# Reading a filter's mirrored rows by DMA from GpSimd's queue instead of turning them on TensorE

## The chip, the cores and the metric

The kernel runs on one core of a Trainium2 chip. The core has TensorE (PE, matrix products; its weight loads are shown as PEld), VectorE (DVE), ScalarE (ACT), GpSimd (POOL) and SyncE (SP), each with an instruction queue of its own that runs in order, and DMA engines that move data between the device memory and the on-chip memory SBUF. TensorE writes to PSUM, from which ScalarE or VectorE copies. The metric is device time in microseconds of one execution. The median of 3 runs of the kernel before is 134.64 us (133.65, 134.64, 134.67).

## The reference

Two branches share the input `x` of 2048 rows by 512 columns (bf16) and are mixed by a gate for each row:

```python
def _A_ref(x, w_r, w_i):                  # spectral filter
    X = rfft2(x.astype(float32), axes=(-2, -1))
    X = X * (w_r + 1j * w_i)              # w_r, w_i: 2048 x 257
    return irfft2(X, s=(S, D), axes=(-2, -1)).astype(bfloat16)

def _B_ref(x, w1, b1, w2, b2):            # MLP over the rows
    h = _layernorm(x, axis=-1)
    u = _gelu(einsum("bsd,sf->bdf", h, w1) + b1)        # f: 1792
    return (einsum("bdf,fs->bds", u, w2) + b2).transpose(0, 2, 1)

g = sigmoid((x * gate_w).sum(-1, keepdims=True))
out = g * _A_ref(A_x, ...) + (1 - g) * _B_ref(A_x, ...)
```

## The kernel before, in words

The MLP is 224 matmuls of 512 columns for `w1` (L656, PSUM tiles `acc` and `fb`), a GELU on ScalarE (L670), and 224 more for `w2` (L932). The Fourier transforms are made of matmuls with tables of cosines and sines and of radix-4 steps on VectorE:

- Over the rows: a radix-4 step on `x` (L494 to L501), then matmuls (`fa`, L513 to L516) with the table `ta`, copied into `X` by ScalarE (L519).
- Over the columns: radix-4 steps on `X` (L526 to L533, L552 to L568), then matmuls (L621 to L624), copied into `B` by ScalarE (L628).
- The product with the filter: sums and differences of `B` (L769, L770), four products with `W` (L777), combinations (L782 to L791). A few lines at the edge of the spectrum are done apart: `sp`/`fx`, `c0`/`cm`/`ce`, `nyq` with the filter row `wn`.
- The inverse: radix-4 steps, matmuls with `ti` (L838 to L845) and then `tg` (L913 to L917), folds (L937 to L941) and the mixing with the MLP's output (L952, L958, L970).

Because the input is real, the product for the spectral row k needs the filter's rows k + 512 e and their mirror images 512 (e + 1) - k, for e = 0 to 3. `W` holds both: `W[p, component, lt, e, s, column]`, with lt = 0 for even rows k and lt = 1 for odd ones, s = 0 for the row itself and s = 1 for its mirror. Before, even rows lie in rising order: partition p below 64 holds k = 4p, the others k = 2 + 4 (p - 64). So the mirrored rows are needed in falling order. For lt = 0 they are loaded in rising order into `wt`, and TensorE turns them with the reversed unit matrix `flip`: eight matmuls of 256 columns (L706) and four of 2 (L716), which ScalarE copies into `W` (L710, L719). For lt = 1 the DMA itself reads rows backwards, 32 at a time:

```python
for e in range(4):
    dma(W[:, 1, e, 1, 0:257], v[:, 3 - e, 3, :].rearrange("(o i) l -> o i l", o=4)[:, ::-1])
```

All filter loads stand on SyncE's queue, 18 for each of the two components (`ld_W`, L413). All DMAs go through the helper `dma` in L303, so all have that line in the profile; its third argument can name another engine's queue. `wprep` (L724) halves the filter's row 0 and makes sums of its end columns; it needs all of `W`.

The order of the work comes from a planner (`Plan`, L137). Each task has an engine, a cost in us, the keys it reads and writes, PSUM tiles to take or give back, and a priority (a smaller number goes first). The planner plays the tasks through with these costs, each engine taking the ready task of the smallest number, and the instructions are issued in the order found. So the order is fixed before the run: an engine that reaches an instruction whose data are not there waits, whatever stands behind it. Waits between engines and DMAs are added by the framework from what the instructions read and write.

SyncE's order around the change: the inputs and first weights, `gw`, the filter's first component (priority 17), four loads of `wb` (22), the second component (25), `ti` (28), `tg` (29), then the loads of `w2` (31 and above).

Of the kernel before, what the change touches and what calls it, by code (L numbers as in the profile page):

```python
# [16 lines left out]
P = 128  # L17
S = 2048
# [12 lines left out]

def ti_at(r):
    return (0, 1024, 512, 1920)[r], (512, 896)[r % 2]


def make_tables():
# [10 lines left out]
    for r in range(4):  # L47
        s = 4 * p + r
        for n, k0 in enumerate((0, 2)):
            th = ang(s, k0 + 4 * np.arange(64), S)  # L50
            ta[:, r, n * 128:n * 128 + 64] = np.cos(th)
            ta[:, r, n * 128 + 64:n * 128 + 128] = -np.sin(th)
        ta[:, r, 64] = alt
# [5 lines left out]
        k = np.where(p < 64, 4 * p, 2 + 4 * (p - 64))  # L59
        o, w = ti_at(r)  # L60
        v = ti[:, o:o + w]
        if r % 2:
            sg = np.where(p < 64, 1.0, -1.0)[:, None]
# [6 lines left out]
            v[0, 2:4] = alt * (0.5 ** 0.5 if r == 1 else -(0.5 ** 0.5))  # L70
# [5 lines left out]
        else:  # L76
            s5 = np.append(s, 512)
            for lt, kk in enumerate((k, 1 + 4 * (p ^ 96))):
                th = ang(kk, s5, S)
                c, n = np.cos(th), -np.sin(th)  # L80
                if lt == 0:
                    n[0, 0:P] = 0.0 if r == 0 else -alt
# [4 lines left out]
    ti[0, 2816:2945] = np.append(alt, 1.0)  # L87
# [174 lines left out]
def kernel(  # L262
# [42 lines left out]
    def alloc_first():  # L305
# [17 lines left out]
        t["wn"] = sb([1, 2, WL], BF16, "wn")  # L323
        t["ta"] = sb([P, 4, 640], BF16, "rot")
        t["wt"] = sb([P, 2, 4, WL], BF16, "wt")
# [87 lines left out]
    def ld_W(comp):  # L413
        v = wsrc[comp].rearrange("(e c k) l -> c e k l", e=4, k=4)
        z = wsrc[comp].rearrange("(v u w) l -> w u v l", v=4, u=2)

        def emit():
            W, u = t["W"][:, comp], t["wt"][:, comp]
            dma(u[64:127, :, 0:257], v[65:128, :, 0, :])
            dma(u[0:64, :, 0:257], v[64:128, :, 2, :])  # L420
            dma(u[127:128, 0:2, 0:257], z[0:1, 1, 2:4, :])
            dma(u[127:128, 2, 0:257], wsrc[comp][1536:1537, :])
            dma(u[127:128, 3, 0:257], wsrc[comp][0:1, :])
            for e in range(4):
                dma(W[:, 1, e, 1, 0:257], v[:, 3 - e, 3, :].rearrange("(o i) l -> o i l", o=4)[:, ::-1])
            for o in range(4):
                dma(W[32 * o:32 * o + 32, 1, :, 0, 0:257], v[96 - 32 * o:128 - 32 * o, :, 1, :])
            dma(W[1:64, 0, :, 0, 0:257], v[1:64, :, 0, :])
            dma(W[64:128, 0, :, 0, 0:257], v[0:64, :, 2, :])
            for i in range(2):  # L430
                dma(W[0:1, 0, 2 * i:2 * i + 2, 0, 0:257], z[0:1, i, 0:2, :])
            dma(t["wn"][:, comp, 0:257], wsrc[comp][1024:1025, :])
        return emit

    for comp in range(2):
        add("SP", 9.0 - 2 * comp, ld_W(comp), writes=[("W", comp), ("wt", comp)], prio=17 + 8 * comp, nbytes=300000, after=[a0])
        if comp == 0:
            load_wb(1)
# [8 lines left out]
    for r in range(4):  # L447
# [60 lines left out]
        for dq in range(4):  # L508
            def fa(r=r, dq=dq):
                pa = t["pa", r, dq] = ps([P, 2, 2, P], F32, "fa", 2)  # L510
                ta = t["ta"][:, r, :]
                w = lambda k: t["xf", r][:, k, dq * P:(dq + 1) * P]
                T.matmul(pa[:, 1], lhsT=w(2), rhs=ta[:, 256:512], start=True, stop=False)  # L513
                T.matmul(pa[:, 1], lhsT=w(3), rhs=ta[:, 384:640], start=False, stop=True)
                T.matmul(pa[:, 0, :, 0:64], lhsT=w(0), rhs=ta[:, 0:128], start=True, stop=True)
                T.matmul(pa[:, 0, :, 64:128], lhsT=w(1), rhs=ta[:, 128:256], start=True, stop=True)  # L516
# [59 lines left out]
    def sp0():  # L576
        V.tensor_copy(t["sp"][:], t["X"][:, 0, :, :, :, 0])
# [25 lines left out]
    add("DVE", 0.15, lambda: V.tensor_copy(t["X"][:, 0, :, :, :, 0], t["fx"][:]), reads=["fx"],  # L603
# [94 lines left out]
    for comp in range(2):  # L698
        for lt in (0,):
            for a in range(2):  # L700
                tag = ("fa", "fb")[a]

                def wf(comp=comp, lt=lt, a=a, tag=tag):
                    pw = t["pw", comp, lt, a] = ps([P, 2, L], F32, tag, 2)
                    for i in range(2):
                        T.matmul(pw[:, i], lhsT=t["flip"][:], rhs=t["wt"][:, comp, 3 - 2 * a - i, 0:L], start=True, stop=True)  # L706
                add("PE", mm(256, 256), wf, reads=[("wt", comp), "flip"], writes=[("pw", comp, lt, a)], prio=5, alloc=[tag])

                def wfe(comp=comp, lt=lt, a=a):
                    A.copy(t["W"][:, comp, lt, 2 * a:2 * a + 2, 1, 0:L], t["pw", comp, lt, a][:])  # L710
                add("ACT", act(512), wfe, reads=[("pw", comp, lt, a)], writes=[("W~", comp, lt)], prio=3, free=[tag])

    def wfn():
        pw = t["pwn"] = ps([P, 4, 2], F32, "fa", 2)
        for e in range(4):
            T.matmul(pw[:, e], lhsT=t["flip"][:], rhs=t["wt"][:, :, 3 - e, 256], start=True, stop=True)  # L716
    add("PE", mm(*[4] * 4), wfn, reads=[("wt", 0), ("wt", 1), "flip"], writes=["pwn"], prio=5, alloc=["fa"])
    wtk = [("W~", comp, 0) for comp in range(2)]
    add("ACT", 0.3, lambda: A.copy(t["W"][:, :, 0, :, 1, 256], t["pwn"][:].rearrange("p e k -> p k e")),  # L719
        reads=["pwn"], writes=wtk, prio=3, free=["fa"])  # L720
# [3 lines left out]
    def wprep():  # L724
        W, pm = t["W"], t["wpm"]
        V.tensor_scalar_mul(W[0:1, :, 0, 0, :, 0:257], W[0:1, :, 0, 0, :, 0:257], 0.5)
# [4 lines left out]
    add("DVE", 0.8, wprep, reads=[], writes=[("W", 0), ("W", 1), "wpm"] + wtk, prio=1)  # L731
# [283 lines left out]
```

## Time and profile before

| | |
|---|---|
| median of 3 runs | 134.64 us |
| the profiled execution, its own time | 134.46 us |
| its span, first to last instruction | 132.6 us |
| PE busy | 124.6 us (94%), 769 matmuls |
| DVE busy | 115.3 us (87%), 295 instructions |
| ACT busy | 80.5 us (61%), 155 instructions |
| POOL busy | 0.2 us, 4 instructions |
| DMA | 23.18 MB, all on the queues of SyncE (q1) and ScalarE (q10) but for code |
| granted TensorE clock | 1.00 throughout |

Times inside the profile are us from the first instruction. "Busy" is the time in which an engine had an instruction running; matmuls overlap, so one of 512 columns is shown with 0.37 us but follows the last by 0.216. The idle time in front of an instruction is put down to what released it: another engine's instruction, a DMA, or "issue". The chain that ended last goes back from the last instruction, at each step to what it waited for. DMA share is the mean busy share of the 16 DMA engines.

### The profile page before, as it was taken

Reading aid. Unit: us, or ns where it says so; the run is one execution under the profiler, and the core shown is the slowest. Engines: PE = TensorE matmul, PEld = TensorE weight load, DVE = VectorE, ACT = ScalarE, POOL = GpSimd, SP = SyncE. Lnnn points to the kernel's source line nnn. Section 1 sums busy time; section 2 is a strip of 40 time slices with the busy share of each in tenths; the row PEclk is TensorE's granted clock in tenths of the full one; section 3 lists DMA queues with packets and bytes.
Section 4 is the critical chain, followed back from the end, with each engine's and each line's share of the span. In section 5 each row is a group of like instructions: output and inputs, shape, how many; then the busy total and the mean of one; then the engine's idle time right before and its main releaser. Section 6 shows DMA issues by size and latency. Waiting matters only on the chain.

```text
span 132.6 us, 2193 instructions
## 1 busy us (share of the span) xinstructions
PE 124.6 (94%) x769; PEld 70.7 (53%) x783; DVE 115.3 (87%) x295; ACT 80.5 (61%) x155; POOL 0.2 (0%) x4
## 2 busy tenths in 40 slices
PE   6749999999999999999999999999999999999991
PEld 2234464545544566744445544556865766655590
DVE  2987999999999997389999999999598599999841
ACT  4036699999999999972222016235994857755200
POOL 0000000000000000000000000000000000000000
PEclk9999999999999999999999999999999999999999
DMA  4899999925499565999964930000000003034031
GB/s 133 245 370 394 393 380 371 321 60 134 90 309 342 96 134 131 337 373 413 421 253 72 420 146 2 0 2 5 0 0 0 5 0 158 23 135 161 2 119 40
DMA packets 17350, 23.18 MB, mean 175 GB/s; under 512 B 1446, under 2 KB 14780, under 8 KB 17340
## 3 DMA queue, kind: packets, MB, share of 16 engines
q1 hardware_dynamic: 16780, 22.39, 49.8%
q10 hardware_dynamic: 560, 0.66, 1.6%
q8 instruction: 6, 0.10, 0.3%
q14 instruction: 4, 0.03, 0.1%
HBM read 20.93 MB, written 2.10 MB: 174 GB/s over the span
## 4 chain that ended last, share of the span: by engine, by line
PE 80%; DVE 10%; DMA 6%; SPq 1%; issue 1%
PE acc L932 35%; PE acc L656 25%; DMA x<-in_A_x_dram 6%; DVE stats L462 4%; PE fb L656 3%; PE fa L838 1%; PE fb L838 1%; PE fa L624 1%; PE fb L624 1%; SPq L303 1%; DVE mv L463 1%; DVE gl L495 1%; DVE st L494 1%; PE fa L513 1%; DVE nmr L477 1%
## 5 line engine op out<-in xcount | busy, mean ns | idle before, releaser
L932 PE MATMUL acc<-gl,wb 128*128 128x512 bf16 (+1 forms) x123 | 30.5, 373 | 0.3
L656 PE MATMUL acc<-h,wb 128*128 128x512 bf16 x124 | 28.8, 379 | 0.2
L932 PE MATMUL acc<-gl,wa 128*128 128x512 bf16 (+1 forms) x94 | 23.2, 372 | 0.1
L932 PEld LDWEIGHTS <-wb 128*128 128x128 bf16 x144 | 14.9, 114 | 10.7 <-DMA wb<-in_B_w_dram 0.6
L952 ACT ACTIVATE x<-acc,ombb,omg 128x512 bf16<-128x512 f32 x14 | 10.7, 778 | 15.5 <-PE acc L932 15.4
L656 PEld LDWEIGHTS <-wb 128*128 128x128 bf16 x128 | 12.4, 97 | 13.5
L656 PE MATMUL acc<-h,wa 128*128 128x512 bf16 x62 | 16.8, 379 | 1.2 <-DVE stats L462 0.7
L932 PEld LDWEIGHTS <-wa 128*128 128x128 bf16 x108 | 11.7, 114 | 8.5
L656 PEld LDWEIGHTS <-wa 128*128 128x128 bf16 x96 | 9.1, 98 | 10.3 <-DMA wa<-in_B_w_dram 0.9
L670 ACT ACTIVATE gl<-acc,b1f 128x512 bf16<-128x512 f32 x12 | 8.5, 708 | 9.6 <-PE acc L656 9.6
L462 DVE BATCH_NORM_STATS2 stats<-x 128x6 f32<-128x512 bf16 x16 | 10.8, 673 | 2.8 <-DMA x<-in_A_x_dram 2.8
L519 ACT CAST X<-fa 128x512 bf16<-128x512 f32 x16 | 8.8, 583 | 3.9 <-PE fa L516 3.8
L486 ACT ACTIVATE h<-x,nmr,rstd 128x512 bf16<-128x512 bf16 x13 | 9.8, 805 | 1.2 <-DVE nmr L477 1.2
L684 ACT ACTIVATE x<-x 128x512 bf16<-128x512 bf16 x16 | 10.2, 672 | 0.0
L923 ACT ACTIVATE eo<-fa,g 128x512 bf16<-128x512 f32 x8 | 5.5, 688 | 6.7 <-DVE x L958 5.0
L656 PE MATMUL fb<-h,wa 128*128 128x512 bf16 x31 | 9.0, 379 | 0.0
L513 PE MATMUL fa<-rot,gl 128*128 128x256 bf16 x16 | 4.3, 272 | 2.1 <-DMA rot<-dft_ta 2.1
L353 PE MATMUL fa<-xp 128*128 128x512 bf16 x13 | 4.4, 514 | 1.2 <-DVE xp L314 1.2
L923 ACT ACTIVATE eo<-fb,g 128x512 bf16<-128x512 f32 x8 | 5.5, 686 | 0.0
L958 DVE TENSOR_TENSOR x<-x,eo 128x512 bf16<-128x512 bf16 x14 | 5.4, 418 | 0.0
L628 ACT CAST B<-fb 128x512 bf16<-128x512 f32 x8 | 5.2, 651 | 0.0
L628 ACT CAST B<-fa 128x512 bf16<-128x512 f32 x8 | 5.1, 639 | 0.0
(170 smaller groups left out, 227.3 us busy)
## 6 DMA issues: line engine op xcount, KB each, us to landing
wb<-in_B_w_dram SPq DMA_DIRECT2D x8, 512.0 KB
wb<-in_B_w_dram SPq DMA_DIRECT2D x4, 1024.0 KB
wa<-in_B_w_dram SPq DMA_DIRECT2D x3, 1024.0 KB
wa<-in_B_w_dram SPq DMA_DIRECT2D x3, 768.0 KB
x<-in_A_x_dram SPq DMA_DIRECT2D x3, 512.0 KB
out_dram<-x SPq DMA_DIRECT2D x3, 512.0 KB
rot<-dft_ti SPq DMA_DIRECT2D x1, 736.5 KB
rot<-dft_ta SPq DMA_DIRECT2D x4, 160.0 KB
```

What stands on the lines that cost most here:

```text
L462: V.bn_stats(out=t["stats"][:, j, :], in_=t["x"][:, j // 4, j % 4, :])
L486: add("ACT", act(512, 2), lambda j=j: A.activation(t["h"][:, j // 4, j % 4, :], t["x"][:, j // 4, j % 4, :], ActF.Identity, bias=t["nmr"][ ...
L513: T.matmul(pa[:, 1], lhsT=w(2), rhs=ta[:, 256:512], start=True, stop=False)
L519: add("ACT", act(512), lambda r=r, dq=dq: A.copy(t["X"][:, :, r, :, dq, :], t["pa", r, dq][:]), reads=[("pa", r, dq)], writes=[("X", r, dq ...
L628: A.copy(t["B"][:, lt, e, 2 * c:2 * c + 2, :].rearrange("p s (i b) -> p s i b", b=4), t["pb", lt, e, c][:].rearrange("p s b i -> p s i b"))
L656: T.matmul(t["u", ft][:], lhsT=w[:, j // 4, j % 4, c * P:(c + 1) * P], rhs=t["h"][:, j // 4, j % 4, :], start=(j == jorder[0]), stop=(j == ...
L670: gelus.append(add("ACT", act(512, 1), lambda ft=ft: A.activation(t["gl"][:, ft, :], t["u", ft][:], ActF.Gelu_apprx_tanh, bias=t["b1f"][:, ...
L684: A.activation(t["x"][:, q, r, :], t["x"][:, q, r, :], ActF.Copy, accum_out=t["glog"][:, 4 * q + r:4 * q + r + 1])
L923: A.activation(t["eo", j][:], t["i3", j][:], ActF.Copy, scale=t["g"][:, j:j + 1])
L932: T.matmul(t["y", j, n][:, cs], lhsT=w[:, o, 512 * q + r:512 * q + 512:4], rhs=t["gl"][:, ft, cs], start=(ft == 0), stop=(ft == NFT - 1))
L952: A.activation(tbuf(j).rearrange("p h d -> p (h d)"), t["y", j, 0][:], ActF.Identity, bias=t["ombb2"][:, j:j + 1], scale=t["omg"][:, j:j + 1])
L958: V.tensor_add(o, o, t["eo", j][:])
```

## The change

The even rows get a new order `KE`: partition p holds the row k = (250 + 2 (p // 32) - 8 (p % 32)) mod 256, that is four runs of 32 falling rows; row 0 comes to lie in partition 96. Now the mirrored even rows rise and are loaded forwards (`y`, SyncE), and the rows themselves fall and are read backwards in four runs of 32. These four loads, and the four of the odd mirrored rows, are issued for each component on GpSimd's queue (`runs`), sixteen in all, behind a small copy that makes GpSimd wait for `X`. SyncE keeps 12 loads for each component, and two that replace values in row 96 are issued after GpSimd's (`special`). The loads of `wt`, the twelve turning matmuls and five copies are gone. The tables `ta` and `ti` follow the new order, and the lines kept apart move from partition 0 to partition 96. The buffer of `wt` is gone; `ze`, which used to share the buffer of `h`, gets one of its own.

```diff
+KE = (250 + 2 * (np.arange(P) // 32) - 8 * (np.arange(P) % 32)) % 256
...
-        for n, k0 in enumerate((0, 2)):
-            th = ang(s, k0 + 4 * np.arange(64), S)
+        for n in range(2):
+            kk = KE.reshape(2, 2, 32)[:, 1 - n].reshape(64)
+            th = ang(s, kk, S)
...
-        t["wn"] = sb([1, 2, WL], BF16, "wn")
+        t["wn"] = sb([P, 2, WL], BF16, "wn")
         t["ta"] = sb([P, 4, 640], BF16, "rot")
-        t["wt"] = sb([P, 2, 4, WL], BF16, "wt")
...
     def ld_W(comp):
         v = wsrc[comp].rearrange("(e c k) l -> c e k l", e=4, k=4)
+        y = wsrc[comp].rearrange("(e c k) l -> c e k l", e=4, k=8)
         z = wsrc[comp].rearrange("(v u w) l -> w u v l", v=4, u=2)
 
         def emit():
-            W, u = t["W"][:, comp], t["wt"][:, comp]
-            dma(u[64:127, :, 0:257], v[65:128, :, 0, :])
-            dma(u[0:64, :, 0:257], v[64:128, :, 2, :])
-            dma(u[127:128, 0:2, 0:257], z[0:1, 1, 2:4, :])
-            dma(u[127:128, 2, 0:257], wsrc[comp][1536:1537, :])
-            dma(u[127:128, 3, 0:257], wsrc[comp][0:1, :])
+            W, src = t["W"][:, comp], wsrc[comp]
+            tiny_ = [(W[96:97, 0, 1:3, 1, 0:257], z[0:1, 0:2, 3, :]), (W[96:97, 0, 0, 1, 0:257], src[0:1, :]),
+                     (W[96:97, 0, 3, 1, 0:257], src[1280:1281, :]), (t["wn"][96:97, comp, 0:257], src[1024:1025, :])]
+            for o in range(4):
+                dma(W[32 * o + o // 3:32 * o + 32, 0, :, 1, 0:257], y[32 + o // 3:64, ::-1, 6 - 2 * o, :])
+                dma(*tiny_[o])
+                dma(W[32 * o:32 * o + 32, 1, :, 0, 0:257], v[96 - 32 * o:128 - 32 * o, :, 1, :])
+
+        def runs():
+            W, src = t["W"][:, comp], wsrc[comp]
+            if comp == 0:
+                nc.gpsimd.tensor_copy(t["wn"][0:1, 0, 0:1], t["X"][0:1, 0, 2, 0, 0, 0:1])
             for e in range(4):
-                dma(W[:, 1, e, 1, 0:257], v[:, 3 - e, 3, :].rearrange("(o i) l -> o i l", o=4)[:, ::-1])
-            for o in range(4):
-                dma(W[32 * o:32 * o + 32, 1, :, 0, 0:257], v[96 - 32 * o:128 - 32 * o, :, 1, :])
-            dma(W[1:64, 0, :, 0, 0:257], v[1:64, :, 0, :])
-            dma(W[64:128, 0, :, 0, 0:257], v[0:64, :, 2, :])
+                dma(W[:, 0, e, 0, 0:257], src[512 * e + 2:512 * e + 258, :].rearrange("(i q z) l -> q z i l", q=4, z=2)[:, 0, ::-1], nc.gpsimd)
+                dma(W[:, 1, e, 1, 0:257], v[:, 3 - e, 3, :].rearrange("(o i) l -> o i l", o=4)[:, ::-1], nc.gpsimd)
+
+        def special():
             for i in range(2):
-                dma(W[0:1, 0, 2 * i:2 * i + 2, 0, 0:257], z[0:1, i, 0:2, :])
-            dma(t["wn"][:, comp, 0:257], wsrc[comp][1024:1025, :])
-        return emit
-
+                dma(t["W"][96:97, comp, 0, 2 * i:2 * i + 2, 0, 0:257], z[0:1, i, 0:2, :])
+        return emit, runs, special
+
+    wtask = {}
     for comp in range(2):
-        add("SP", 9.0 - 2 * comp, ld_W(comp), writes=[("W", comp), ("wt", comp)], prio=17 + 8 * comp, nbytes=300000, after=[a0])
+        wtask[comp] = ld_W(comp)
+        add("SP", 5.0, wtask[comp][0], writes=[("W", comp, 0)], prio=17 + 8 * comp, nbytes=530000, after=[a0])
...
+                pe = pa[:, 0].rearrange("p c (h o i) -> p c h o i", h=2, o=2)
...
-                T.matmul(pa[:, 0, :, 0:64], lhsT=w(0), rhs=ta[:, 0:128], start=True, stop=True)
-                T.matmul(pa[:, 0, :, 64:128], lhsT=w(1), rhs=ta[:, 128:256], start=True, stop=True)
+                T.matmul(pe[:, :, :, 1], lhsT=w(0), rhs=ta[:, 0:128], start=True, stop=True)
+                T.matmul(pe[:, :, :, 0], lhsT=w(1), rhs=ta[:, 128:256], start=True, stop=True)
...
     for comp in range(2):
-        for lt in (0,):
-            for a in range(2):
-                tag = ("fa", "fb")[a]
...
-                        T.matmul(pw[:, i], lhsT=t["flip"][:], rhs=t["wt"][:, comp, 3 - 2 * a - i, 0:L], start=True, stop=True)
...
-                    A.copy(t["W"][:, comp, lt, 2 * a:2 * a + 2, 1, 0:L], t["pw", comp, lt, a][:])
...
-            T.matmul(pw[:, e], lhsT=t["flip"][:], rhs=t["wt"][:, :, 3 - e, 256], start=True, stop=True)
...
+        add("POOL", 8.0, wtask[comp][1], reads=[("X", 2, 0)], writes=[("W", comp, 1)], prio=comp, nbytes=526336)
+        add("SP", 1.0, wtask[comp][2], reads=[("W", comp, 0)], writes=[("W", comp, 1), ("W", comp)], prio=29.5, nbytes=4112)
...
-        V.tensor_scalar_mul(W[0:1, :, 0, 0, :, 0:257], W[0:1, :, 0, 0, :, 0:257], 0.5)
+        V.tensor_scalar_mul(W[96:97, :, 0, 0, :, 0:257], W[96:97, :, 0, 0, :, 0:257], 0.5)
...
-                        t["ze"] = sb([P, 2, 2, 2, 2, L], BF16, "h")
+                        t["ze"] = sb([P, 2, 2, 2, 2, L], BF16, "ze")
```

Lines of `sp0`, `fx`, `nyq`, `lines` and the store back into `B` change in the same way, index 0 to 96.

## The prediction

> **What bounds the kernel now.** I read the page's table of engines first, then the stretches (busy time by stage), then the chain that ended last in order of time, then the instructions of VectorE and of SyncE around the filter `W`.
>
> The stretches give, for each piece of the span, its length and the busy time of PE, PEld, DVE, ACT and POOL, then clock, DMA share and GB/s:
>
> ```profile
> 24.00:46.00 22.00, 21.89 (x122) 11.14 (x123) 21.65 (x52) 21.61 (x49) 0.00 (x0) 1.00 0.68 190
> 46.00:57.00 11.00, 10.89 (x91) 7.40 (x91) 7.64 (x23) 10.98 (x25) 0.00 (x0) 1.00 0.70 203
> ...
> 70.50:91.00 20.50, 20.39 (x98) 10.58 (x99) 20.30 (x22) 5.72 (x8) 0.00 (x0) 1.00 0.30 104
> ```
>
> From 24 us on TensorE has no hole (21.89 of 22.0, 10.89 of 11.0, 20.39 of 20.5), at a granted clock of 1.00. So what leaves TensorE's queue shortens the kernel, as long as VectorE, nearly as full (21.65 of 22.0), does not become late. ScalarE is full as well until 57.
>
> The chain, in order of time, carries the turning matmuls themselves:
>
> ```profile
> 35.99 0.22 PE fa L706 x2
> ...
> 36.64 0.33 PE fb L706 x2
> ...
> 49.20 0.38 PE fa L706 x2
> ...
> 49.80 0.22 PE fb L706 x2
> ...
> 50.24 0.08 PE fa L716 x4
> ```
>
> VectorE where it first touches the filter (start, busy, and in brackets the idle time before and what ended it):
>
> ```profile
> 51.60 0.24 DVE L603 CAST X<-fx 128x32 bf16<-128x32 f32 x1
> 52.52 0.42 DVE L726 TENSOR_SCALAR W<-W 1x1028 bf16<-1x1028 bf16 x1 [0.68 <-DMA W<-in_A_w_i_dram]
> ...
> 53.86 0.17 DVE L763 TENSOR_TENSOR ce<-cm 128x8 f32<-128x8 f32 x1
> 56.20 0.17 DVE L740 CAST c<-B 128x8 f32<-128x8 bf16 x1 [2.18 <-ACT B L628]
> 56.70 0.17 DVE L741 CAST c<-B 128x8 f32<-128x8 bf16 x1 [0.32 <-ACT B L628]
> 56.78 1.22 DVE L769 TENSOR_TENSOR xp<-B 128x2048 bf16<-128x2048 bf16 x1
> ```
>
> This is VectorE's only hole in the middle of the kernel. `wprep` (L726 to L730) and the small products after it (L758 to L763) take 52.52 to 54.03, 1.5 us, inside it; the next instruction waits until 56.20 for ScalarE's copies of `B`. So `wprep` could start as late as 56.20 - 1.5 = **54.7** and nothing would move.
>
> **Part by part.**
>
> *Turning matmuls gone.* The chain's rows: 0.22 + 0.33 + 0.38 + 0.22 + 0.08 = **1.23 us**. Without the gaps that stand in two of them it is 8 x 0.11 + 0.08 = 0.96. I take 1.2, because the gaps come with the switch of weights to `flip`. At the other end of the kernel, VectorE must let it through: its last instruction but the final four ends at 125.6, and the next sits idle 1.04 us for TensorE (126.65), and the last three wait 0.78, 0.30 and 0.43 more. So VectorE can give 1.04 us at once and the last three pieces the rest.
>
> *Turning copies gone.* ScalarE loses four copies of 0.61 to 0.72 us and one of 0.35 (L710, L719), about 2.5 us of issue in stretches where it is full. Three of the five lie at 50.2 to 52.1. The next `B` copies start at 52.65 because VectorE finishes their data at 51.84 (L603) and TensorE its matmuls thereafter, and those eight copies set 56.20. So ScalarE's gain is worth nothing to the end: it lies between two copies that wait for others.
>
> *SyncE's queue.* Before, 18 filter loads for each component, median 0.53 us an issue, from 21.70 to 34.66 and from 37.37 to 51.05 with the waits between them; only then come `ti`, `tg` and the first `w2` loads (52.07). Now 12 for each and 2 late ones: 12 x 0.53 = 6.4 us, twice, around the 2.6 us of the four `wb` loads, so `ti` stands at about 21.7 + 6.4 + 2.6 + 6.4 = 37, to 43 with the 5.7 us in which these issues waited for `wb` data. All of this is earlier than now and hidden: the first `w2` matmul is at 70.46. One of the new loads has 31 rows. [...]
>
> *The late special loads.* They overwrite row 96 after GpSimd's loads of it, so SyncE must wait for these to land. Behind that wait stand the `w2` loads: three of 1 MB at the 343 GB/s of the stretch 57 to 70.5 are 9.2 us, so SyncE may stand there until about 61 before TensorE is short at 70.46. `ti` and `tg` stand ahead of it (priorities 28 and 29 against 29.5).
>
> *Sixteen loads on GpSimd: the unknown.* The trace has four instructions on that engine and no DMA of its. It starts after the first copy of the third quarter of `X` (L519, 23.32 + 0.56 = 23.9), with its own small copy at about 24.1. Call d the time for one load, by issue or by draining. The second component's have landed at 24.1 + 16d + 1.5 (1.5 is from the end of the last issue, 51.05, to 52.52 where L726 ran); then two special issues of 0.35 and their landing: 0.7 + 1.5. `wprep` can start at **27.8 + 16d**, and with 54.7 this gives the point from which it decides: d = **1.68 us**.
>
> Rows for d. A filter load on SyncE issues in 0.53: `wprep` ready at 36.3. Four such reversed loads per component stand on SyncE's queue now, and where three of them drain almost alone the stretch reads
>
> ```profile
> 28.00:30.00 2.00, 2.00 (x11) 0.88 (x9) 2.00 (x5) 1.98 (x3) 0.00 (x0) 1.00 0.13 34
> ```
>
> 13% of sixteen engines, 34 GB/s: 64.2 KB at 34 GB/s are 1.9 us. If all sixteen drained one behind another like that, d = 1.9 and `wprep` is ready at 58.2. The longest spacing of reversed loads on SyncE is 2.15 us (issued at 40.43, 42.58, 44.73, with waits for `wb` data between): 62.2. I take d = 1.0, nearer to the issue row than to the draining row, since the 13% is about two engines' worth and the other engines stood idle, so loads spread over several would overlap: `wprep` ready at 43.8, eight us before VectorE gets there.
>
> [...]
>
> *Where `wprep` stands.* VectorE runs in the planner's order. With the planner's costs followed by hand (8 us for eight GpSimd loads, 5 for SyncE's twelve), the late loads end at about 51 of its clock, after L603 (48) and before the next instruction that waits for `B` (53). So it stays in the hole. Were it put behind, about 1.4 us would come onto VectorE's path.
>
> *Costs at nothing.* Row numbers, tables and partition 96 instead of 0 keep instruction shapes and counts; the interleaved writes of L515 and L516 keep their 128 columns. `ze` gets its own buffer: its first copy is at 91.16 and the last reader of `h` at 70.4, so no wait goes.
>
> Sum: 132.6 - 1.2 = 131.4 us span, with the 1.86 outside it 133.26 against the profiled 134.46. The median of the runs shown is 0.18 above the profiled one: **133.4**.
>
> **Rivals.**
>
> *A. GpSimd's loads are late (slower).* Place: `wprep` at the head of VectorE's queue. Behind it stand the products with the filter (62.10), then everything of the inverse transform, for which TensorE waits in order (first at 90.78). Above d = 1.68 each us that `wprep` is late goes to the end, less the 1.2. At d = 1.9: 58.2 - 54.7 = 3.5 late, 134.64 - 1.2 + 3.5 = 136.9. At d = 2.15: 7.5 late, 140.9. If GpSimd advanced only while VectorE is idle, it would start in earnest where VectorE stands still at 51.84: 51.84 + 16 x 0.53 + 3.7 = 64.0, 9.3 late, 142.7. For it: VectorE is 98% busy from 24 to 46. Against: nothing in the trace ties the two engines.
>
> [...]
>
> *B. The gain does not reach the end.* TensorE comes 1.2 us earlier to L842 at 90.78, whose data come from VectorE's chain and SyncE's 8 KB store to `B` (issued at 88.04), neither of which moves. Unless the planner puts five or six more matmuls of 0.216 ahead of it, TensorE waits there: 134.6. For it: VectorE's 20.30 of 20.5. Against: the planner sees the same thing and places them.
>
> *C. VectorE is slowed by GpSimd* (the other direction of A): if each of sixteen issues held it for 0.53, that is 8.5 us before 51.84, and at worst 134.64 - 1.2 + 8.5 = 141.9.
>
> That the loads fall apart into small pieces is unlikely: eight of the same form run now, at 64.2 KB.
>
> **How the numbers follow.** Forecast 0.50 (132.5 to 134.0, the spread being 0.96 against 1.23 and some half us of re-placed gaps), B 0.21 (134.0 to 135.2), A 0.23, C 0.06. 1% is 1.35 us and about what a measurement tells from no change (the three runs before span 1.0). The forecast's centre lies at -0.9%, so it is split: 0.32 faster by over 1%, 0.18 within; B adds 0.20 within and 0.01 slower. Faster 0.32, same 0.38, slower 0.30. The range goes from 132.5 to 140.9, the bound at d = 2.15; beyond it lie the worst of A and C, and the lowest order effects, together about 0.15.
>
> **What would show it.** Right: no rows of L706 to L720; POOL's sixteen issues from about 24 to 40; L726's counterpart starting about 51.9 without a wait; the 56.78 product unmoved; TensorE with no hole and an end 1.2 earlier. Wrong: an idle of VectorE before `wprep` released by a DMA of `W`, or one of TensorE before the first matmul of L621 or L842.

## The result and the profile after

The changed kernel takes 140.76 us (median of 6, 140.51 to 142.01), the kernel before 134.45 (median of 6 beside it, 133.65 to 134.95). The ratio is 1.049, with a 95% interval from 1.044 to 1.055: **slower by 6.3 us**. The forecast was 133.4 us and a little faster; its range, 132.5 to 140.9, just holds the time. The profiled execution took 140.63 us with a span of 138.6, so 6.0 more span than before.

The new kernel's lines have other numbers: 4 higher up to the loads of the filter, then 11 higher, and 9 lower behind the place where the turning stood. `dma` is L307, the copy of `fx` L614, the copies into `B` L639, `wprep` L717 to L721, the sums L760 and L761, the products L768, the first matmuls of the inverse transform L833 to L836, `w2` L923.

The first two stretches as before, then two behind 70, with the same columns (POOL, the fifth busy time, was 0.00 before):

```profile
24.00:46.00 22.00, 21.89 (x122) 11.17 (x123) 21.69 (x51) 21.70 (x51) 10.42 (x16) 1.00 0.97 204
46.00:57.00 11.00, 10.89 (x80) 6.71 (x80) 6.03 (x16) 10.28 (x23) 0.00 (x0) 1.00 0.49 127
70.00:80.00 10.00, 7.78 (x36) 3.73 (x35) 9.90 (x9) 0.00 (x0) 0.00 (x0) 1.00 0.64 238
80.00:98.00 18.00, 14.82 (x70) 7.56 (x70) 17.86 (x18) 5.81 (x8) 0.00 (x0) 0.98 0.01 2
```

Up to 57 TensorE is as full as it was. Behind 70 it now has holes, 2.2 us in the first of these stretches and 3.2 in the second; before, it had 0.1 us between 70.5 and 91. VectorE is full in both, so it is VectorE's work that came late. Where it came late is seen on VectorE (start, busy, and in brackets the idle time before and what ended it):

```profile
51.09 0.24 DVE L614 CAST X<-fx 128x32 bf16<-128x32 f32 x1
...
55.82 0.17 DVE L731 CAST c<-B 128x8 f32<-128x8 bf16 x1 [3.56 <-ACT B L639]
...
56.96 1.22 DVE L760 TENSOR_TENSOR xp<-B 128x2048 bf16<-128x2048 bf16 x1
...
64.91 0.43 DVE L717 TENSOR_SCALAR W<-W 1x1028 bf16<-1x1028 bf16 x1 [5.60 <-DMA W<-in_A_w_i_dram]
...
69.65 2.29 DVE L768 TENSOR_TENSOR xp<-xp,W 128x4096 bf16<-128x4096 bf16 x1
```

The first product with the filter before:

```profile
62.10 2.27 DVE L777 TENSOR_TENSOR xp<-xp,W 128x4096 bf16<-128x4096 bf16 x1
```

Two things differ from before. `wprep` (L717) no longer stands in the hole behind L614 but behind the sums. And there it waits **5.60 us for a DMA of `W`**, the second component. The first product starts at 69.65 instead of 62.10, 7.55 us late. The transfer in question is found on SyncE's queue (start of the first issue, time to the end of the last, tile, count):

```profile
40.65 10.70 SPq L307 DMA_DIRECT2D W<-in_A_w_i_dram  x10
51.40 1.71 SPq L307 DMA_DIRECT2D wn<-in_A_w_i_dram  x1
53.15 0.32 SPq L307 DMA_DIRECT2D W<-in_A_w_i_dram  x1
53.57 0.37 SPq L307 DMA_DIRECT2D rot<-dft_ti  x1
53.98 0.43 SPq L307 DMA_DIRECT2D tg<-dft_tg  x1
54.51 0.38 SPq L307 DMA_DIRECT2D wa<-in_B_w_dram  x1
55.00 1.29 SPq L307 DMA_DIRECT2D W<-in_A_w_r_dram  x2
57.14 0.38 SPq L307 DMA_DIRECT2D wa<-in_B_w_dram  x1
57.63 1.23 SPq L307 DMA_DIRECT2D W<-in_A_w_i_dram  x2
```

`ti` (rot) is issued at 53.57, later than the 51.15 of before, although twelve loads stand ahead of it for each component where there were eighteen. The four special loads of row 96 (the two lines "W x2") come only behind `ti`, `tg` and, in the planner's order, between the 1 MB loads of `w2`. The last pair is issued by 58.86 and frees VectorE at 64.91, 6.05 us later.

In the chain that ended last, in order of time, the rows of L706 and L716 are gone, and these loads have come in, where TensorE stood before:

```profile
40.65 10.04 DMA W<-in_A_w_i_dram
50.71 0.31 SPq L307
51.06 6.06 DMA W<-in_A_w_i_dram
57.14 0.38 SPq L307
57.63 7.09 DMA W<-in_A_w_i_dram
64.91 0.09 DVE W L717
```

These rows also tell what SyncE stands waiting for. The load issued at 40.65 lands 10.04 us later, at 50.69, and the eighth load behind it is issued at 50.71. The load of 31 rows, issued at 51.06, lands 6.06 us later, and the eighth load behind it, one of `w2`, is issued at 57.14. In this trace SyncE's loads signal eight semaphores in turn and wait on them in the same turn, so an issue stands until the load eight before it has landed.

The fifth to the eighth load of the second component wait in this way for the four of `wb` that stand ahead of it. SyncE's waits for `wb` between 21 and 54 (us in all, times, longest), first before, then after:

```profile
SPq L303 <- DMA wb<-in_B_w_dram: 5.7, 4, 1.6
...
SPq L307 <- DMA wb<-in_B_w_dram: 8.4, 6, 2.2
```

So half the filter's bytes left SyncE's queue, and the queue was no quicker. In the stretch from 24 to 46, where GpSimd's loads now run beside SyncE's, the share of time in which the DMA engines were busy is 0.97 instead of 0.68 (the last number but one in the rows of the stretches). That GpSimd's loads make `wb` land later fits these figures.

GpSimd, which was the open question of the prediction, is not late with its own loads. Its rows, in the same form:

```profile
23.44 0.18 POOL L433 COPY wn<-X 1x1 bf16<-1x1 bf16 x1 [23.00 <-ACT X L530]
23.56 5.49 POOL L307 DMA_DIRECT2D W<-in_A_w_r_dram  x8
32.50 0.68 POOL L307 DMA_DIRECT2D W<-in_A_w_i_dram  x1 [3.45 <-DMA W<-in_A_w_r_dram]
33.48 4.69 POOL L307 DMA_DIRECT2D W<-in_A_w_i_dram  x7 [0.30 <-DMA W<-in_A_w_r_dram]
```

Sixteen issues, all but the first of 0.68 us, are over at 38.2, with VectorE busy 21.69 of 22.0 in that stretch. And the gain that was forecast is there for a while, as TensorE's rows show:

```profile
68.99 1.46 PE L923 MATMUL acc<-gl,wa 128*128 128x512 bf16 x6
...
72.61 0.62 PE L923 MATMUL acc<-gl,wb 128*128 128x512 bf16 x2 [1.73 <-DMA wb<-in_B_w_dram]
...
76.70 1.05 PE L923 MATMUL acc<-gl,wb 128*128 128x512 bf16 x4 [0.44 <-DMA wb<-in_B_w_dram]
...
97.72 0.27 PE L833 MATMUL fa<-rot,B 128*128 128x129 bf16 x1 [3.13 <-DMA B<-s]
```

The first `w2` matmul before:

```profile
70.30 1.46 PE L932 MATMUL acc<-gl,wa 128*128 128x512 bf16 x6
```

It starts at 68.99 against 70.30: 1.31 us gained. Then TensorE waits 1.73 + 0.44 = 2.2 us for `w2` loads, which sit on the same late queue, and 3.13 us before the inverse transform for the end of VectorE's chain.

**The account on VectorE** closes within 0.2 us. Its first product is 7.55 late. Before, it waited for TensorE ahead of the four last pieces, 1.04 + 0.78 + 0.30 + 0.43 = 2.55 us; now only 0.17 of that is left, so 2.38 are absorbed. A wait for ScalarE in the inverse transform grew from 1.2 to 1.9. 7.55 - 2.38 + 0.7 = 5.9 us; the last piece starts at 135.40 instead of 129.74, 5.66 late. The other 0.34 of the span lies behind it.

### The profile page after: what moved, and what is told of

It is laid out like the page before. It is cut to its first block, busy times and chain, and to the rows that moved or that the text cites. A ratio compares the mean times of both kernels' runs of the same rounds, so it can differ in the third digit from the quotient of the medians.

```text
span 138.6 us, 2189 instructions
## 1 busy us (share of the span) xinstructions
PE 125.8 (91%) x757; PEld 70.5 (51%) x771; DVE 115.3 (83%) x295; ACT 78.4 (57%) x150; POOL 11.2 (8%) x21
## 4 chain that ended last, share of the span: by engine, by line
DMA 35%; PE 27%; DVE 21%; SPq 12%; issue 2%; DVEq 0%
PE acc L923 18%; DMA W<-in_A_w_i_dram 17%; SPq L307 12%; DMA wa<-in_B_w_dram 11%; DMA W<-in_A_w_r_dram 6%; DVE xp L768 3%; DVE st L768 3%; DVE xp L773 2%; DVE B L780 2%; DVE xp L774 2%; PE fa L829 2%; DMA B<-s 1%; PE fb L829 1%; DVE X L741 1%; DVE st L564 1%
## 5 line engine op out<-in xcount | busy, mean ns | idle before, releaser
L923 PE MATMUL acc<-gl,wb 128*128 128x512 bf16 (+1 forms) x123 | 31.0, 377 | 2.3 <-DMA wb<-in_B_w_dram 2.2
L667 PE MATMUL acc<-h,wb 128*128 128x512 bf16 x124 | 28.2, 379 | 0.2
L923 PE MATMUL acc<-gl,wa 128*128 128x512 bf16 (+1 forms) x94 | 23.2, 372 | 0.2
L923 PEld LDWEIGHTS <-wb 128*128 128x128 bf16 x144 | 14.9, 115 | 13.2 <-DMA wb<-in_B_w_dram 3.1
L923 PEld LDWEIGHTS <-wa 128*128 128x128 bf16 x108 | 11.6, 114 | 8.6
L307 POOL DMA_DIRECT2D W<-in_A_w_i_dram x8 | 5.4, 677 | 3.7 <-DMA W<-in_A_w_r_dram 3.7
L307 POOL DMA_DIRECT2D W<-in_A_w_r_dram x8 | 5.5, 694 | 0.0
L639 ACT CAST B<-fa 128x512 bf16<-128x512 f32 x8 | 5.0, 628 | 0.5 <-PE fa L635 0.5
```

The lines of the kernel that those rows point to most:

```text
L307: (eng or nc.sync).dma_start(out=out_ap, in_=in_ap)
L639: A.copy(t["B"][:, lt, e, 2 * c:2 * c + 2, :].rearrange("p s (i b) -> p s i b", b=4), t["pb", lt, e, c][:].rearrange("p s b i -> p s i b"))
L667: T.matmul(t["u", ft][:], lhsT=w[:, j // 4, j % 4, c * P:(c + 1) * P], rhs=t["h"][:, j // 4, j % 4, :], start=(j == jorder[0]), stop=(j == ...
L923: T.matmul(t["y", j, n][:, cs], lhsT=w[:, o, 512 * q + r:512 * q + 512:4], rhs=t["gl"][:, ft, cs], start=(ft == 0), stop=(ft == NFT - 1))
```

## The experiments

The theory from these rows: the special loads on SyncE's queue make `W` late, and this is nearly the whole loss. The rivals: SyncE's queue is late because of the load with 31 rows; `wprep`'s place behind the sums costs it; GpSimd's queue costs it. All times are medians; ratios are to the kernel before on the same chip. In the kernels with other line numbers the lines are named as they stand there.

**What the turning is worth.** From the kernel before, the twelve turning matmuls and five copies were taken out, the mirrored even rows being loaded straight into `W` in rising order and used unturned, so the output is not the reference's. `wprep` was kept in its place.

```diff
-            W, u = t["W"][:, comp], t["wt"][:, comp]
+            W, u = t["W"][:, comp], t["W"][:, comp, 0, :, 1, :]
...
-                        T.matmul(pw[:, i], lhsT=t["flip"][:], ...
-                    A.copy(t["W"][:, comp, lt, 2 * a:2 * a + 2, 1, 0:L], ...
```

> The kernel before with the turning left out: the mirrored even rows are loaded straight into W, rising, so the product uses them in the wrong order; the twelve turning matmuls and five copies are gone, every load keeps its place and count, and the halving of row 0 keeps its place on VectorE. If the turning cost the 1.2 us of its rows in the chain: ratio 0.988 to 0.993, 133.2. Rival (the gain is lost at the first matmul of the inverse transform, which waits for VectorE): 134.2 to 134.7, ratio 0.998 to 1.002.

Measured: 133.69 us against 134.16, ratio 0.9958 [0.9929, 0.9986], so 0.56 us (0.2 to 0.95) are gained, not 1.2. TensorE at its first `w2` matmul:

```profile
68.98 1.46 PE L910 MATMUL acc<-gl,wa 128*128 128x512 bf16 x6
```

VectorE at the first of its last pieces, here and in the kernel before:

```profile
125.82 0.75 DVE L948 SCALAR_TENSOR_TENSOR x<-acc,omg,x 128x512 bf16<-128x512 f32 x1 [0.18 <-PE acc L910]
...
126.65 0.75 DVE L970 SCALAR_TENSOR_TENSOR x<-acc,omg,x 128x512 bf16<-128x512 f32 x1 [1.04 <-PE acc L932]
```

At the first `w2` matmul 1.32 us are gained (68.98 against 70.30). Of this, 0.83 arrives at the last pieces (125.82 against 126.65): the 1.04 us in which VectorE stood idle there have shrunk to 0.18, and VectorE's own work sets the rest.

**The special loads on GpSimd's queue.** One edit in the changed kernel:

```diff
-                dma(t["W"][96:97, comp, 0, 2 * i:2 * i + 2, 0, 0:257], z[0:1, i, 0:2, :])
+                dma(t["W"][96:97, comp, 0, 2 * i:2 * i + 2, 0, 0:257], z[0:1, i, 0:2, :], nc.gpsimd)
...
-        add("SP", 1.0, wtask[comp][2], ...
+        add("POOL", 1.0, wtask[comp][2], ...
```

> The changed kernel with one edit: the four late special loads of row 96 are issued on GpSimd's queue behind its sixteen loads, not on SyncE's between the megabyte loads of w2. Queue theory (the filter is late because the special loads reach the head of SyncE's queue late, at 55.0 to 58.9 us, and then land behind the w2 loads already handed to the same rings, 6 us after their issue): VectorE's wait of 5.6 us for W before the halving of row 96 falls below 1 us, the first product with W starts at 64 to 65 instead of 69.65, and the time falls from 140.8 to 134.5 to 136. GpSimd theory (its sixteen loads themselves are late): the special loads wait for the same loads, the wait stays at 5 us or more, 140 to 141.

Measured: 136.61 us, ratio 1.0154 [1.0091, 1.0217]: 4.15 of the 6.3 us are back from four loads of 1 KB changing queue. There is no wait for `W` at `wprep`; the first product:

```profile
63.48 2.29 DVE L768 TENSOR_TENSOR xp<-xp,W 128x4096 bf16<-128x4096 bf16 x1
```

6.17 earlier than in the changed kernel, still 1.4 later than before. The time came out a little above what was expected; TensorE still waits 1.54 us for a `wb` load at 71.92. The queue theory holds for most of the loss.

**The load with 31 rows in two, 16 + 15.** Everything else as in the changed kernel:

```diff
-                dma(W[32 * o + o // 3:32 * o + 32, 0, :, 1, 0:257], y[32 + o // 3:64, ::-1, 6 - 2 * o, :])
+                if o < 3:
+                    dma(W[32 * o:32 * o + 32, 0, :, 1, 0:257], y[32:64, ::-1, 6 - 2 * o, :])
+                else:
+                    dma(W[97:113, 0, :, 1, 0:257], y[33:49, ::-1, 0, :])
+                    dma(W[113:128, 0, :, 1, 0:257], y[49:64, ::-1, 0, :])
```

> The changed kernel with one edit: the load of 31 rows of each component is cut into one of 16 and one of 15. One-ring theory (31 rows go through a single DMA engine, whose ring fills, so the one-row load of wn behind it takes 4.25 and 1.71 us to issue): wn issues in under 0.6 us, SyncE reaches ti at about 47 instead of 53.6 us, the special loads land about 5 us earlier, VectorE's wait of 5.6 us falls below 1.5, and the time is 135 to 136.5. Rival (SyncE is held by its eight loads in flight, each issue waiting for the eighth before it to land): wn issues fast, but ti moves by less than 2 us and the time stays at 139 to 141.

Measured: 137.54 us, ratio 1.0218 [1.0159, 1.0278]. SyncE's queue:

```profile
39.28 11.93 SPq L307 DMA_DIRECT2D W<-in_A_w_i_dram  x11
51.25 0.25 SPq L307 DMA_DIRECT2D wn<-in_A_w_i_dram  x1
...
51.97 0.37 SPq L307 DMA_DIRECT2D rot<-dft_ti  x1
```

VectorE at `wprep`:

```profile
61.83 0.43 DVE L721 TENSOR_SCALAR W<-W 1x1028 bf16<-1x1028 bf16 x1 [2.13 <-DMA W<-in_A_w_i_dram]
```

The small `wn` load behind the split one issues in 0.25 us instead of 4.25 (first component) and 1.71 (second). So behind a 31-row load the next issue stands, and with the split it does not. In the changed kernel from 53 to 54 us, while the second component's 31-row load (issued at 51.06, landed at 57.12) was on its way, the DMA engines' busy share was 0.07 at 20 GB/s, 1.1 engines' worth of sixteen. That a single engine moved it fits this share; that its ring filled is the author's reading, and no run shows it. But `ti` moves only from 53.57 to 51.97, and the second component's loads take as long as before (12.6 us for thirteen against 12.8 for twelve): the rival reading, that the waits for the load eight before hold SyncE, is right as well. The time lies between the two expectations. It is 3.2 us lower because the last special pair is issued by 56.58 instead of 58.86 and frees VectorE 5.25 us later instead of 6.05.

**The special loads ahead of `w2`, still on SyncE.** The `w2` loads were made to wait for them in the order; the planner then puts `wprep` back in the hole by itself.

```diff
-            add("SP", 0.01, w2alloc, writes=[("w2a", k)], prio=31 + i, alloc=["wa" if k == 0 else "wb"])
+            add("SP", 0.01, w2alloc, writes=[("w2a", k)], prio=31 + i, alloc=["wa" if k == 0 else "wb"], after=sptask)
```

> The changed kernel with one edit: all w2 loads stand behind the special loads on SyncE's queue (and the planner then puts the halving of row 96 before the sums of B, not after them). Queue theory: the special loads are issued at about 54 to 55.5, behind ti and tg only, and land by 58; VectorE waits for them about 4 to 6 us from 51.8, goes on with the sums at about 59, and starts the first product at 63.5 to 65 instead of 69.65; 134.5 to 136.5. GpSimd theory: landing stays at 62 or later and the time at 139 or more.

Measured: 139.23 us, ratio 1.0386 [1.0328, 1.0443]. VectorE at `wprep` and at the first product:

```profile
62.01 0.43 DVE L719 TENSOR_SCALAR W<-W 1x1028 bf16<-1x1028 bf16 x1 [9.10 <-DMA W<-in_A_w_i_dram]
...
69.18 2.29 DVE L770 TENSOR_TENSOR xp<-xp,W 128x4096 bf16<-128x4096 bf16 x1
```

The numbers are those set for the GpSimd theory (landing at 62 or later, 139 us or more), but its reason is not seen: GpSimd's sixteen issues are over at 38.5 in this kernel too. The queue theory's own figures, special loads issued by 55.5, did not come out. Ahead of the megabytes the last special pair lands 2.3 us after its issue (59.70 to 62.01) instead of 6.05, so standing behind `w2` costs 3.7 us. But SyncE gets to it only at 57.26, hardly earlier than the 57.63 of the changed kernel, and `wprep`, now first in VectorE's order, makes the sums wait too. The queue is late ahead of `w2` already.

**The sixteen reversed loads back on SyncE**, the new row order kept:

```diff
-                dma(W[:, 1, e, 1, 0:257], v[:, 3 - e, 3, :].rearrange("(o i) l -> o i l", o=4)[:, ::-1], nc.gpsimd)
+                dma(W[:, 1, e, 1, 0:257], v[:, 3 - e, 3, :].rearrange("(o i) l -> o i l", o=4)[:, ::-1])
...
-        add("POOL", 8.0, wtask[comp][1], reads=[("X", 2, 0)], writes=[("W", comp, 1)], prio=comp, nbytes=526336)
+        add("SP", 4.0, wtask[comp][1], reads=[("W", comp, 0)], writes=[("W", comp, 1)], prio=17.5 + 8 * comp, nbytes=526336)
```

> The changed kernel with its sixteen reversed loads back on SyncE's queue, behind each component's twelve, and nothing on GpSimd: renumbering without the other queue. If GpSimd's queue takes work from SyncE that counts: SyncE has 22 filter loads for each component in place of 14, ti is issued at 57 to 62, VectorE's wait for W grows to 6 to 10 us, 141 to 146. If the rings' rate sets it and GpSimd brings nothing: 139 to 141, as the changed kernel.

Measured: 150.27 us, ratio 1.111 [1.101, 1.121]. SyncE's queue:

```profile
53.95 0.37 SPq L307 DMA_DIRECT2D rot<-dft_ti  x1
...
57.69 7.59 SPq L307 DMA_DIRECT2D W<-in_A_w_i_dram  x8
...
67.10 2.72 SPq L307 DMA_DIRECT2D W<-in_A_w_i_dram  x2
```

GpSimd's queue is worth 9.5 us to this row order. Ahead of `ti` it gains next to nothing: `ti` is issued at 53.95 with eight loads more ahead of it on SyncE's queue, against 53.57. In return SyncE waits 4.5 us for `wb` between 21 and 54 instead of 8.4, and the DMA engines' busy share from 24 to 46 is 0.66 instead of 0.97. This is the trace's sign that GpSimd's loads delay SyncE's. The loss of this kernel lies behind `ti`, where SyncE has no room for the other eight loads. There SyncE's own time, waits for landing included, is what counts: the second component's eight loads alone hold SyncE for 7.59 us.

**All three mends together**: special loads on GpSimd, the 31 rows split, and `wprep` tied behind L614 into the hole (with 5.5 us instead of 8 as the planner's cost of GpSimd's eight loads).

```diff
-        add("POOL", 8.0, wtask[comp][1], ...
+        add("POOL", 5.5, wtask[comp][1], ...
...
-    add("DVE", 0.8, wprep, reads=[], writes=[("W", 0), ("W", 1), "wpm"], prio=1)
+    add("DVE", 0.8, wprep, after=[fxt], reads=[], writes=[("W", 0), ("W", 1), "wpm"], prio=1)
```

> All three mends together: special loads on GpSimd's queue, the 31 rows in 16 and 15, the halving in VectorE's hole. If late loads and place are the whole cause: no wait of VectorE for W that reaches the sums of B, ti issued by 52.5, no wait of TensorE for wb over 0.5 us, first product at 62 and the time that of the kernel before with the turning left out, 133.7 (133.2 to 134.4). If GpSimd's queue costs something else besides: 135 or more.

Measured: 134.59 us against 134.36, ratio 1.0019 [0.9986, 1.0052]. The loss is gone within the interval, though the time is a little above the 133.2 to 134.4 expected. VectorE at `wprep` and at the first product:

```profile
54.30 0.19 DVE L725 TENSOR_TENSOR wpm<-W 128x16 f32<-128x16 bf16 x1 [1.01 <-DMA W<-in_A_w_i_dram]
...
62.40 2.29 DVE L772 TENSOR_TENSOR xp<-xp,W 128x4096 bf16<-128x4096 bf16 x1
```

TensorE in the first stage of `w2`:

```profile
71.99 0.63 PE L927 MATMUL acc<-gl,wb 128*128 128x512 bf16 x2 [0.88 <-DMA wb<-in_B_w_dram]
```

GpSimd at its last special load, which waits for the reversed loads to land:

```profile
46.22 0.50 POOL L307 DMA_DIRECT2D W<-in_A_w_i_dram  x1 [5.92 <-DMA W<-in_A_w_i_dram]
```

The product is within 0.3 us of its old place. The 0.5 us that the turning is worth do not show: TensorE gives 0.88 back waiting for `wb`.

The same **without the split**, so against the last kernel:

```diff
-                if o < 3:
-                    ...
+                dma(W[32 * o + o // 3:32 * o + 32, 0, :, 1, 0:257], y[32 + o // 3:64, ::-1, 6 - 2 * o, :])
```

> The special loads on GpSimd's queue, as in the run that moved only them, and in the planner GpSimd's eight loads cost 5.5 us in place of 8.0 and the halving of row 96 follows the copy of the edge lines, so that it stands in VectorE's hole before the sums of B. Place theory (behind the sums, the halving and the products of one edge line cost VectorE 1.4 to 1.9 us): the first product with W starts at 61.5 to 62.5 in place of 63.48, the time is 1 to 2 us below the 136.6 of that run: 134.5 to 135.5. Rival (W is not complete by 54, so VectorE waits in the hole and the sums come later): idle of 1 us or more before the halving that passes 54.7, no gain, 136 to 138.

Measured: 136.48 us, ratio 1.0154 [1.0113, 1.0195], the same as with `wprep` behind the sums. Its profiled execution took 140.18 us, 3.7 above the median, so its rows are not compared in time; in it `wn` again took 3.86 and 1.83 us to issue. Putting `wprep` in the hole gains nothing while the 31 rows stand whole, as the rival had it.

**The eight loads of one or two rows on GpSimd's queue too**, on top of the three mends:

```diff
-                dma(*tiny_[o])
...
+                dma(*tiny_[e], nc.gpsimd)
```

> The three mends, and the eight loads of one or two rows moved to GpSimd's queue as well, so SyncE issues nine filter loads for each component. In-flight theory (SyncE may have eight loads in flight, so each filter load takes the time of the eighth before it to land, about 1 us a load whatever its size): SyncE reaches ti about 6 to 8 us earlier than with them, at 44 to 46; 133 to 134. Rival (the rings' rate for 514-byte rows sets it, not the number of loads): ti moves by less than 2 us.

Measured: 136.59 us, ratio 1.0177 [1.0094, 1.026]. `ti` goes from 52.65 to 47.81, so eight loads less are worth 4.8 us to SyncE, 0.6 each. But GpSimd now issues 28 loads, the last at 52.93, and VectorE waits at `wprep`, in the hole, beyond its end (L721 is there the line of `wprep`):

```profile
56.59 0.43 DVE L721 TENSOR_SCALAR W<-W 1x1028 bf16<-1x1028 bf16 x1 [3.16 <-issue]
```

The profile names no releaser ("issue"), but the last load of `W` had been issued 3.1 us before, at 53.45. The lateness has most likely changed queue.

**The price of `wprep`'s place**, measured twice. First in the kernel before, all else kept (the task of the sums is only defined earlier, so that `wprep` can name it):

```diff
-    add("DVE", 0.8, wprep, reads=[], writes=[("W", 0), ("W", 1), "wpm"] + wtk, prio=1)
+    add("DVE", 0.8, wprep, after=[sums], reads=[], writes=[("W", 0), ("W", 1), "wpm"] + wtk, prio=1)
```

> The kernel before, its filter loads, turning matmuls and all else kept, with one change of order: wprep (and with it the small products after it) is put behind the sums of B instead of ahead of them. It measures the place alone. Theory (the place costs): 1.5 us of small instructions leave VectorE's hole and stand between the sums and the first product, so this product starts 1.4 to 1.9 us later than 62.10, at 63.5 to 64.0; VectorE's chain carries that to the inverse transform's matmuls, and the time is 1.3 to 1.9 over the kernel before, 135.7 to 136.3. Rival (the delay is taken up by idle time of VectorE between 62 and 90): less than 0.5 over, below 134.9.

Measured: 134.29 us against 134.33, ratio 0.999 [0.9962, 1.0018]. The theory fell: the product is 1.1 us later (63.21), a little less than it said, and it costs nothing. VectorE at the first product and at its last pieces:

```profile
63.21 2.27 DVE L780 TENSOR_TENSOR xp<-xp,W 128x4096 bf16<-128x4096 bf16 x1
...
127.13 1.21 DVE L973 SCALAR_TENSOR_TENSOR x<-acc,omg,x 128x512 bf16<-128x512 f32 x2
```

VectorE carries the delay to the end, where the 1.04 us of idle time ahead of the last pieces are gone: they took it up. TensorE has no hole either, because the planner, which knows of this delay, puts more `w2` matmuls ahead of the inverse transform (first at 91.80 instead of 90.62).

Then with the special loads on GpSimd and the split, `wprep` left where the planner puts it; against the kernel with all three mends:

```diff
-        add("POOL", 5.5, wtask[comp][1], ...
+        add("POOL", 8.0, wtask[comp][1], ...
...
-    add("DVE", 0.8, wprep, after=[fxt], reads=[], writes=[("W", 0), ("W", 1), "wpm"], prio=1)
+    add("DVE", 0.8, wprep, reads=[], writes=[("W", 0), ("W", 1), "wpm"], prio=1)
```

> The changed kernel with the special loads on GpSimd's queue and the 31-row load split in 16 + 15 rows, but with wprep where the planner puts it by itself, behind the sums. Against the kernel that has these two and wprep in the hole (134.59) it measures the place a second time. Theory: no wait for W, first product at 63.4 to 64.0, time 135.9 to 136.5, 1.3 to 1.9 over 134.59. Rival (what was left in the kernel with special loads on GpSimd alone, 136.61, was the one-engine load and its blocked queue, not the place): 134.6 to 135.2.

Measured: 135.29 us, ratio 1.0046 [1.0013, 1.008]. By the ratios this is 0.4 us over the kernel with all three mends, 1.0019 [0.9986, 1.0052], and the intervals overlap. Against 136.61 with the special loads alone, the split is worth about 1.3 us. Neither expectation was met exactly, the rival's only just not (134.6 to 135.2): the place costs less than 1.3 to 1.9.

**`ti` and `tg` behind the first five `w2` loads**, on top of the three mends (both tasks were made to depend on the fifth):

```diff
+        if i == 4:
+            ti_task.deps.add(w2_task)
+            tg_task.deps.add(w2_task)
```

> The kernel with all three mends (134.59), with the tables ti and tg (0.92 MB) issued behind the first five loads of w2 instead of ahead of them. There TensorE waits 0.88 us for a wb load at 71.99. Theory (that load is late because 0.92 MB stand ahead of it, 2.7 us at 343 GB/s): the wait is gone, the first matmul of the inverse transform comes 0.5 to 0.9 earlier than 91.66, and the time is 133.7 to 134.1, at or a little below the kernel before. Rival (the wb load waits for its buffer, whose last reader among the w1 matmuls sets its issue at 55.6): the wait stays above 0.6 and the time within 0.2 of 134.6.

Measured: 134.46 us, ratio 0.9987 [0.9958, 1.0016]. The wait at the first `wb` tile is gone, and 0.54 us of it come back at the next one, while VectorE waits 2.0 us for `W` in the hole. TensorE:

```profile
75.19 1.05 PE L930 MATMUL acc<-gl,wb 128*128 128x512 bf16 x4 [0.54 <-DMA wb<-in_B_w_dram]
```

The wait went as the theory said, the time stayed where the rival had put it, and no version of the change was shown to beat the kernel before. In one table (times in us; "product" is the start of the first product with the filter):

| kernel | wait for `W` | product | `ti` issued | time | ratio |
|---|---|---|---|---|---|
| before | 0.68, in the hole | 62.10 | 51.15 | 134.45 | 1 |
| changed | 5.60 | 69.65 | 53.57 | 140.76 | 1.0494 |
| special loads on GpSimd | none | 63.48 | 52.58 | 136.61 | 1.0154 |
| 31 rows split | 2.13 | 66.63 | 51.97 | 137.54 | 1.0218 |
| these two | none | 63.66 | 51.28 | 135.29 | 1.0046 |
| and `wprep` in the hole | 1.17, in the hole | 62.40 | 52.65 | 134.59 | 1.0019 |
| before, `wprep` behind the sums | none | 63.21 | 51.45 | 134.29 | 0.9990 |
| before, no turning | 0.27, in the hole | 61.90 | 50.52 | 133.69 | 0.9958 |

## Why the prediction was wrong, by its own steps

- *Turning matmuls gone*: the mechanism was right and the size off. TensorE reaches the first `w2` matmul 1.3 us earlier, as 1.23 us of chain rows said. At the end of the kernel it is 0.56 us (0.2 to 0.95), not 1.2. The step assumed that behind the 1.04 us of VectorE's idle time the last pieces would give the rest; they gave nothing.
- *Turning copies gone, worth nothing*: no run speaks against it. The wait for `B` behind L614 is still there, and ends at 55.82 instead of 56.20.
- ***SyncE's queue* failed.** It counted issues, 12 x 0.53, added the 5.7 us of waits for `wb` that it saw before, and put `ti` at 37 to 43; it was issued at 53.57. Before, 18 loads took 13 to 14 us with the waits between. Twelve loads with half the bytes took 13.3 and 12.8. The step left out that an issue waits for the load eight before it to land, and priced the effect of GpSimd's loads on SyncE's at nothing. With them in flight the waits for `wb` grew to 8.4 us, and the DMA engines' busy share from 24 to 46 rose from 0.68 to 0.97. And the load of 31 rows held the next issue for 4.25 and 1.71 us, and the second component's took 6.06 to land; in `ti`'s 37 to 43 the step has no term for it beyond one issue of 0.53.
- ***The late special loads* failed on the same ground.** With `ti` at 53.57, the special loads were issued at 55.0 to 58.9. The step gave them 1.5 us to land, taken from a row where the first 1 MB load behind was issued only at 52.07; between megabytes they took 6.05. The deadline it set for SyncE, 61, was one for the `w2` matmuls; the deadline that decided was `W`'s own, 54.7.
- *Sixteen loads on GpSimd* was right in its outcome, that GpSimd's own loads are in time, with the terms off in both directions. An issue took 0.68 us where 1.0 was taken for d; but the second component's loads took 6.5 us (median) from issue to landing where the step had 1.5. With the mends GpSimd waited for them until 46.22. By the step's own sum that is d = 1.3, (46.2 - 24.1 - 1.5) / 16, below the point of decision, 1.68. So rival A, GpSimd late, did not happen, and C, VectorE slowed, neither: the product takes 2.29 us against 2.27 to 2.28. Nor did GpSimd stand while VectorE worked: eight loads took 5.49 us of issue, 0.68 to 0.81 each, while VectorE was busy 5.28 of these 5.49 us. That the total landed near the 140.9 of d = 2.15 is a coincidence, and the range held the time for the wrong reason.
- *Where `wprep` stands* failed twice over. It went behind the sums, because the planner starts GpSimd's loads at 31 of its clock: the last writer of the key they read, `("X", 2, 0)`, is a radix-4 step on VectorE and not ScalarE's copy, which the step took. And "about 1.4 us would come onto VectorE's path" was no cost: the delay alone is 1.1 us and adds nothing to the time.
- *B, the gain does not reach the end*: with the mends that is how the change ends, though by other waits, for `wb` and at VectorE's end.
- *What would show it wrong*: an idle of VectorE before `wprep` released by a DMA of `W` was named, and is the line of 5.60. The cause that the prediction hung on it, GpSimd's loads landing late, was not it.

The rival that was missing is a simple one: the last piece of `W` is no longer among the sixteen loads that were weighed, but among the four of 1 KB that have to follow them, and those were put on SyncE's queue, behind `ti`, `tg` and a `w2` load.

## What to carry to other kernels

When a tile is filled by several loads, find the one that is issued last and follow its own queue to its landing; here four loads of 1 KB at the end of a late queue cost most of 6.3 us, and the sixteen of 64 KB on a queue of their own were in time. Price a DMA queue by the pace of its rows in the same stretch, waits included, not by issues times the median issue (twelve loads took 13.3 and 12.8 us, not 6.4), and look at what the other queues have in flight in that stretch (here the DMA engines' busy share rose from 0.68 to 0.97). And one piece of idle time at an engine's end, VectorE's 1.04 us here, can pay for one delay or carry one gain, not both.

## What was not expected of the hardware

- Behind a 31-row load of 62 KB the next issue on its queue took 0.97 to 4.25 us wherever the load stood whole; split in 16 and 15 rows, the next issue takes 0.23 to 0.25.
- A 1 KB load pair landed 2.3 us after its issue ahead of the 1 MB loads and 6.05 us among them, on the same queue.
- In the 3.13 us in which TensorE stood idle before L833, its granted clock fell to half, at 97.2, and stayed there until 100.6. The stretch from L833 on, with the columns of the stretches above (the clock is the third number from the end):

```profile
97.72:100.70 2.98, 2.98 (x17) 2.06 (x18) 2.83 (x5) 1.07 (x2) 0.00 (x0) 0.52 0.03 5
```

The 17 matmuls from L833 on took 3.01 us instead of 1.83, another 1.2 us on TensorE. With the special loads ahead of `w2` it stood idle for 3.17 us and came back at 1.00. With the 31 rows split it stood idle for only 2.07 us and slowed all the same: its matmuls of 128 columns, 0.06 us apart at 94.69, were 0.11 apart from 95.16 on (mean granted clock of the span 0.987). So in these runs the length of the pause alone does not tell whether the clock falls; what does was not shown.
